# Weights joined in their load buffers, and lower halves of weights and values taken on GpSimd, in a pooled attention and bilinear MoE kernel

## The chip, the cores and the metric

The kernel runs on one core of a Trainium2 chip. The metric is the device time of one launch, in microseconds, as the median of several runs. The engines are TensorE (PE, matrix products; its weight loads are listed as PEld), VectorE (DVE), ScalarE (ACT), GpSimd (POOL) and SyncE (SP), which issues all DMAs here.

## The reference

```python
def _attn_ref(q, k, v):                      # (4, 8, 1152, 64) each, float32
    B, H, S, D = q.shape
    q_pool = q.reshape(B, H, S // 2, 2, D).mean(axis=3)
    scores = 1.0 / np.sqrt(D) * np.matmul(q_pool, k.transpose(0, 1, 3, 2))
    scores = scores - np.max(scores, axis=-1, keepdims=True)
    attn = np.exp(scores)
    attn = attn / (np.sum(attn, axis=-1, keepdims=True) + 1e-09)
    return np.matmul(attn, v).astype(np.float32)

def _moe_ref(x, w_a, w_b, w_out):            # x (2304, 512); weights float64,
    a = x @ w_a                              # (512, 1536), (512, 1536), (1536, 512)
    b = x @ w_b
    return (a * b @ w_out).astype(np.float32)

x = attn_out.transpose(0, 2, 1, 3).reshape(B * S // 2, H * D)
```

The weights arrive as float64. The kernel gets them as pairs of 32-bit words, and has to make numbers of its own formats from the two words of each.

## The kernel before

**Attention.** Work goes by pairs of heads, four to a batch, four batches. For batch 0 there are two rounds over its pairs (even rows, then odd rows); the other batches take each pair in one pass. A pass makes score blocks of 128 rows by 1152 keys on PE (`qk`; float32 for batches 0 and 1, pairs of float16 halves for 2 and 3), 144 blocks in all. `sm_max` (L750) copies a block out of PSUM on DVE and takes its maximum, `sm_exp` (L757) takes the exponent on ACT, `sm_hi` (L770, ACT) and `sm_lo` (L774, DVE) write the upper and lower float16 half of the probabilities, a DMA transposes them, and `pv` (L868) multiplies them with the halves of v. The first four passes go another way: PE transposes the float32 probabilities itself (`tr_pe`, `pv_f`). The halves of v for a pass are made from `vraw` by `v_hi` (L550, ACT) and `v_lo` (L553, DVE) into the one buffer `vs`.

**Weights.** There are 12 slices f of 128 hidden units, each with a tile of a (m = 0), of b (m = 1) and of w_out (m = 2), 512 elements a partition. For each tile SP loads the raw words into one of four buffers (`w_load`), ACT writes the scaled upper word into a separate tile z (`w_abs`, L580) and turns the lower word into the last bits (`w_tail`, L588, in place), POOL adds the sign (`w_sign`, L592), DVE joins the parts in z (`w_join`, L599) and takes the maximum (`w_mag`, L583). For a and b, `w_sum` adds the maxima over the partitions on PE, `w_scale` (L614) and `w_inv` make a scale of them, and `w_hi` (L675, ACT) and `w_lo` (L678, DVE) write the scaled upper and lower halves. For w_out the halves wait for `wo_scale`, which needs all 12 tiles.

**MoE.** The 2304 tokens form nine tiles of 256. For a tile, each f is one step: `moe_mm` (L949) makes a and b in PSUM with 24 products of halves, ACT copies a out (`moe_a`, L984), DVE multiplies (`moe_g`, L987), ACT and POOL split the result into halves (`moe_gh`, L992; `moe_gl`, L995; on DVE for the last three tiles) and `moe_o` (L1014) multiplies with w_out. The steps of tiles that are ready stand between attention's blocks on PE.

**Order.** Each piece of work is a task of class `Plan`, with an engine and names that it reads and writes. The order of each engine is written out by hand in `ORDERS`, five lists of task numbers. Each engine's queue runs in that order.

Of the kernel before, what the change touches and what calls it, by code (L numbers as in the profile page):

```python
# [217 lines left out]


class Plan:  # L220

# [4 lines left out]

    def add(self, eng, dur, key, fn, args=(), r=(), w=(), gen=0.45, block=0.0, port=None, lag=0.0, after=(), mode=0, leaves=None):  # L230
# [1035 lines left out]
```

## Time and profile before

| | us |
|---|---|
| median of 3 runs | 824.34 |
| lowest and highest | 820.56, 826.82 |
| the profiled execution | 820.92 |
| its span, first to last instruction | 819.1 |
| busy: PE, DVE, ACT, POOL | 759.3, 643.9, 567.4, 204.3 |

The span is that of one execution. Busy time counts an instruction from start to end; matmuls overlap each other, so a stretch in which PE is busy throughout can still have room. The mean granted clock of TensorE over the span is 0.977 of full speed.

### The profile page before, as it was taken

Reading aid. Unit: us, or ns where it says so; the run is one execution under the profiler, and the core shown is the slowest. Engines: PE = TensorE matmul, PEld = TensorE weight load, DVE = VectorE, ACT = ScalarE, POOL = GpSimd, SP = SyncE. Lnnn points to the kernel's source line nnn. Section 1 sums busy time; section 2 is a strip of 40 time slices with the busy share of each in tenths; the row PEclk is TensorE's granted clock in tenths of the full one; section 3 lists DMA queues with packets and bytes.
Section 4 is the critical chain, followed back from the end, with each engine's and each line's share of the span. In section 5 each row is a group of like instructions: output and inputs, shape, how many; then the busy total and the mean of one; then the engine's idle time right before and its main releaser. Section 6 shows DMA issues by size and latency. Waiting matters only on the chain.

```text
span 819.1 us, 21402 instructions
## 1 busy us (share of the span) xinstructions
PE 759.3 (93%) x8906; PEld 566.6 (69%) x8906; DVE 643.9 (79%) x1271; ACT 567.4 (69%) x940; POOL 204.3 (25%) x182
## 2 busy tenths in 40 slices
PE   7888457999999999999999999989999999999998
PEld 5665335787678775678658875867678668577775
DVE  5999999899988899999989999979788832321222
ACT  5999987688977788887878789876776752221211
POOL 4787774202311114200240204021310120000000
PEclk9998888999999999999999999999999999999999
DMA  7766778999999999999999999998897670000010
GB/s 253 268 216 206 213 225 190 175 216 193 221 188 213 178 197 195 199 201 207 192 197 168 211 209 184 196 184 175 139 179 121 128 144 2 1 26 1 1 27 26
DMA packets 316433, 132.32 MB, mean 162 GB/s; under 512 B 300848, under 2 KB 302896, under 8 KB 316336
## 3 DMA queue, kind: packets, MB, share of 16 engines
q1 hardware_dynamic: 316336, 130.96, 77.4%
q8 instruction: 69, 1.13, 0.6%
q14 instruction: 28, 0.23, 0.1%
HBM read 50.72 MB, written 4.72 MB: 68 GB/s over the span
## 4 chain that ended last, share of the span: by engine, by line
PE 32%; DVE 22%; DMA 4%; issue 4%; ACT 2%; ACTq 0%; DVEq 0%
PE ab L949 17%; DVE p L774 7%; DVE s L750 6%; PE ab L1014 5%; DMA pt<-p 4%; PE xps L868 3%; PE sps L1014 3%; PE sps L720 3%; ACT p L770 1%; DVE vs L553 1%; DVE g L987 1%; PE xps L1014 1%; DVE vmx L506 1%; DVE kmx L433 1%; DVE k L459 1%
## 5 line engine op out<-in xcount | busy, mean ns | idle before, releaser
L949 PEld LDWEIGHTS <-wab 128*128 128x128 f16 x2592 | 251.1, 98 | 37.5 <-issue 2.1
L949 PE MATMUL ab<-xt,wab 128*128 128x256 f16 x2304 | 262.6, 273 | 0.6 <-DVE o L1020 0.4
L774 DVE SCALAR_TENSOR_TENSOR p<-s,st,p 128x1152 f16<-128x1152 f32 x128 | 183.2, 1436 | 13.4 <-ACT p L770 12.9
L770 ACT ACTIVATE p<-s,st 128x1152 f16<-128x1152 f32 x128 | 158.9, 1249 | 49.2 <-DMA pt<-p 13.6
L757 ACT ACTIVATE s<-s,st 128x1152 f32<-128x1152 f32 x144 | 180.1, 1251 | 17.5 <-DVE s L750 16.3
L868 PE MATMUL xps<-pt,vs 128*64 128x128 f16 (+1 forms) x3888 | 110.1, 216 | 4.9 <-issue 2.0
L868 PEld LDWEIGHTS <-vs 128*64 128x64 f16 x3888 | 101.7, 111 | 17.2 <-issue 14.9
L750 DVE TENSOR_SCALAR_CACHE_REDUCE s<-sps 128x1152 f32<-128x1152 f32 x72 | 96.4, 1348 | 14.1 <-PE sps L718 13.9
L718 PE MATMUL sps<-k,q 64*128 64x512 f32 (+2 forms) x480 | 97.9, 542 | 10.3 <-DVE s L750 6.3
L750 DVE TENSOR_SCALAR_CACHE_REDUCE s<-sps,ksc 128x1152 f32<-128x1152 f32 x72 | 100.8, 1409 | 7.5 <-PE sps L720 6.5
L984 ACT ACTIVATE g<-ab 128x256 f32<-128x256 f32 x108 | 40.2, 375 | 95.2 <-PE ab L949 94.9
L995 POOL TENSOR_TENSOR gl<-g,gh 128x256 f16<-128x256 f32 x72 | 60.0, 839 | 181.3 <-ACT gh L992 153.3
L987 DVE SCALAR_TENSOR_TENSOR g<-ab,cc,g 128x256 f32<-128x256 f32 x108 | 51.2, 478 | 65.7 <-ACT g L984 65.6
L1014 PE MATMUL ab<-wo,gh 128*128 128x512 f16 x336 | 100.2, 380 | 1.6 <-DVE g L987 1.5
L718 PEld LDWEIGHTS sps<-k,q 64*128 64x128 f32 (+1 forms) x480 | 63.9, 190 | 45.0 <-issue 23.3
L592 POOL TENSOR_SCALAR raw<-raw 128x512 f16<-128x512 f32 x36 | 84.7, 2354 | 35.0 <-ACT raw L588 19.4
L992 ACT ACTIVATE gh<-g 128x256 f16<-128x256 f32 x108 | 43.2, 408 | 46.9 <-PE ab L1014 20.4
L720 PE MATMUL sps<-k,q 64*128 64x512 f16 (+2 forms) x720 | 66.9, 327 | 4.8 <-DVE s L750 4.2
L1014 PEld LDWEIGHTS <-gh 128*128 128x128 f16 x432 | 40.1, 100 | 41.6 <-issue 1.5
L430 POOL TENSOR_TENSOR q<-qraw 128x576 f32<-128x576 f32 (+2 forms) x20 | 27.6, 1382 | 150.5 <-PE sps L718 55.5
L1014 PE MATMUL ab<-wo,gl 128*128 128x512 f16 x168 | 63.7, 379 | 0.8 <-POOL gl L995 0.7
L720 PEld LDWEIGHTS <-q 64*128 64x128 f16 (+1 forms) x720 | 41.1, 97 | 32.8 <-issue 13.2
(126 smaller groups left out, 753.6 us busy)
## 6 DMA issues: line engine op xcount, KB each, us to landing
raw<-in_w_ab_dram SPq DMA_DIRECT2D x24, 512.0 KB, 4.2
k<-in_k_dram SPq DMA_DIRECT2D x18, 576.0 KB, 5.2
vraw<-in_v_dram SPq DMA_DIRECT2D x17, 576.0 KB, 4.5
qraw<-in_q_dram SPq DMA_DIRECT2D x12, 576.0 KB, 5.1
...
pt<-p SPq DMA_TRANSPOSE x128, 5.4
...
```

The costliest lines, as they stand in the source:

```text
L592: nc.gpsimd.tensor_scalar(out=raw_h[ri(n)], in0=raw_t[ri(n)][:, :, 1].bitcast(F32), scalar1=2.0 ** -100, scalar2=None, op0=ALU.mult)
L718: return nc.tensor.matmul(out, q, k, start=True, stop=True)
L720: return nc.tensor.matmul(out, q[:, hq], k[:, hk], start=(hq, hk) == (0, 0), stop=(hq, hk) == (1, 0))
L750: nc.vector.tensor_scalar(out=s_t[sbuf(i)], in0=sps[:, at:at + S], scalar1=-1.0 / 16.0 if u is None else ksc[:, u, 4:5], scalar2=None, op0 ...
L757: nc.scalar.activation(out=s, in_=s, func=AF.Exp, scale=-1.0, bias=t[:, 0:1], accum_out=t[:, 1:2])
L770: nc.scalar.activation(out=p_t[pbuf(i)][:, 0], in_=s_t[sbuf(i)], func=AF.Copy, scale=st_t[i % NST][:, 3:4])
L774: nc.vector.scalar_tensor_tensor(out=p[:, 1], in0=s, scalar=st_t[i % NST][:, 3:4], in1=p[:, 0], op0=ALU.mult, op1=ALU.subtract)
L868: nc.tensor.matmul(xps[half(e), at:at + w], vs[:, c, e, hv], pt[t][:, hp, c, c0:c0 + w], start=(c == 0 and n == 0), stop=(c == NCH - 1 and ...
L949: nc.tensor.matmul(dst if t < 8 else dst.rearrange("p (b n) -> p b n", b=B), wab[:, f, 1 - m, a, c], moe_x(t, b, c), start=(n == 0), stop= ...
L987: nc.vector.scalar_tensor_tensor(out=g_t[:, f], in0=ab[j][:, 0], scalar=cc[:, t, f:f + 1], in1=g_t[:, f], op0=ALU.mult, op1=ALU.mult)
L995: (nc.vector if dve else nc.gpsimd).tensor_tensor(out=gl_t[j], in0=g_t[:, f], in1=gh_t[j], op=ALU.subtract)
L1014: nc.tensor.matmul(out_bank(t, u), g[:, us], wo[:, f, a], start=(first and n == 0), stop=(last and n == 2))
```

## The change

**Weights.** The z tiles are gone, and there are seven raw buffers (two of them in the space of an x tile that is not yet in use). `w_mag` takes the maximum of the raw upper words as they were loaded; `w_real` turns it into the real one with two small operations; the scale is a power of 256 that `w_scale` makes from the exponent bits of the sum; `w_z` (ACT) multiplies the upper words by it in place; `w_join` joins in the raw buffer. The joined number is already scaled, so `w_hi` copies and `w_lo` subtracts: for a and b `w_lo` is a `tensor_tensor` on GpSimd. All tiles of a and b come before all of w_out.

**Values.** `v_mul` multiplies `vraw` by its scale in place on GpSimd, `v_hi` copies, `v_lo` is a subtraction on GpSimd.

**Order.** All five lists of `ORDERS` are new, as are some of the planner's durations; the product buffer `xps` gets its dependencies from the order of PE's list.

```diff
 ORDERS = (
     (
-        2, 3, 4, 21, 22, 5, 6, 47, 33, 35, 37, 7, 39, 41, 8, 9, 62, 156, 64, 16, 66, 68, 70, 43, 44, 167, 181, 169,
+        2, 3, 4, 5, 6, 21, 22, 7, 8, 47, 33, 35, 37, 106, 39, 41, 9, 62, 64, 138, 68, 66, 70, 149, 151, 163, 153, 43,
...
-    NRAW, NT_ = 4, 2 * B + 1
+    NRAW, NT_ = 7, 2 * B + 1
...
-    raw_t = [T(f"raw{j}", [128, 512, 2], I32) for j in range(NRAW)]
+    raw_t = [T(f"raw{j}", [128, 512, 2], I32) for j in range(NRAW - 2)]
+    raw_t += [xt[1][:, a].rearrange("p c n -> p (c n)").bitcast(I32).rearrange("p (n w) -> p n w", w=2) for a in range(2)]
...
+    def v_mul(p):
+        nc.gpsimd.tensor_scalar(out=vraw, in0=vraw, scalar1=vsc[:, p, 0:1], scalar2=None, op0=ALU.mult)
+
     def v_hi(p):
-        nc.scalar.activation(out=vs[:, :, :, 0], in_=v_heads, func=AF.Copy, scale=vsc[:, p, 0:1])
+        nc.scalar.activation(out=vs[:, :, :, 0], in_=v_heads, func=AF.Copy)
 
     def v_lo(p):
-        nc.vector.scalar_tensor_tensor(
-            out=vs[:, :, :, 1], in0=v_heads, scalar=vsc[:, p, 0:1], in1=vs[:, :, :, 0], op0=ALU.mult, op1=ALU.subtract
-        )
+        nc.gpsimd.tensor_tensor(out=vs[:, :, :, 1], in0=v_heads, in1=vs[:, :, :, 0], op=ALU.subtract)
...
     def prep_v(p, key):
-        add("ACT", 1.146, key, v_hi, (p,), r=["vraw", f"vsc{p}"], w=["vsh"])
-        add("DVE", 1.36, key, v_lo, (p,), r=["vraw", "vsh", f"vsc{p}"], w=["vsl"], port=True)
+        add("POOL", 2.4, key, v_mul, (p,), r=[f"vsc{p}"], w=["vraw"])
+        add("ACT", 1.146, key, v_hi, (p,), r=["vraw"], w=["vsh"])
+        add("POOL", 2.5, key, v_lo, (p,), r=["vraw", "vsh"], w=["vsl"])
...
-    def w_abs(f, m, n):
-        nc.scalar.activation(out=zt(f, m), in_=raw_t[ri(n)][:, :, 1].bitcast(F32), func=AF.Abs, scale=2.0 ** -112)
...
+    def w_z(f, m, n):
+        by = wz[:, 1, m, f:f + 1].bitcast(F32) if m < 2 else 2.0 ** -112
+        up = raw_t[ri(n)][:, :, 1].bitcast(F32)
+        nc.scalar.activation(out=up, in_=up, func=AF.Copy, scale=by)
...
     def w_join(f, m, n):
-        z = zt(f, m).bitcast(I32)
         nc.vector.scalar_tensor_tensor(
-            out=z, in0=z, scalar=3, in1=raw_t[ri(n)][:, :, 0], op0=ALU.logical_shift_left, op1=ALU.bitwise_or
+            out=zt(f, m).bitcast(I32), in0=raw_t[ri(n)][:, :, 1], scalar=3, in1=raw_t[ri(n)][:, :, 0],
+            op0=ALU.logical_shift_left, op1=ALU.bitwise_or
         )
...
+LO_ON = ("POOL", "POOL")
...
     def w_lo(f, m):
+        if m < 2:
+            on = nc.gpsimd if LO_ON[m] == "POOL" else nc.vector
+            on.tensor_tensor(out=w_dst(f, m, 1), in0=w_src(f, m), in1=w_dst(f, m, 0), op=ALU.subtract)
+            return
         nc.vector.scalar_tensor_tensor(
-            out=w_dst(f, m, 1), in0=w_src(f, m), scalar=w_by(f, m), in1=w_dst(f, m, 0), op0=ALU.mult, op1=ALU.subtract
-        )
+            out=w_dst(f, m, 1), in0=w_src(f, m), scalar=wr[:, 2, f:f + 1], in1=w_dst(f, m, 0), op0=ALU.mult, op1=ALU.subtract
+        )
...
     def prep_w(f, key):
-        for m in range(3):
...
         for m in range(2):
+            prep_raw(f, m, key)
...
     def prep_wo(key):
+        for f in range(NF):
+            prep_raw(f, 2, key)
+            prep_z(f, 2, key)
```

GpSimd's order before, in the rows up to the second lower half of g (`gl`). The names `raw`, `xt`, `xr` and `q` are the raw words, the halves of x and the pooled queries.

```order
L592 TENSOR_SCALAR raw_99<-raw_99 128x512
L909 TENSOR_TENSOR xt_63<-x_66,xt_63 128x256
L592 TENSOR_SCALAR raw_100<-raw_100 128x512
L592 TENSOR_SCALAR raw_101<-raw_101 128x512
L592 TENSOR_SCALAR raw_102<-raw_102 128x512
L430 TENSOR_TENSOR q_79<-qraw 128x320
L909 TENSOR_TENSOR xr<-x_66,xr 128x64
L909 TENSOR_TENSOR xt_63<-x_66,xt_63 128x256
L995 TENSOR_TENSOR gl_90<-g,gh_92 128x256
L430 TENSOR_TENSOR q_78<-qraw 128x576
L995 TENSOR_TENSOR gl_91<-g,gh_93 128x256
```

GpSimd's order now, in the rows up to the first `gl`. L620 is `w_sign`, L714 `w_lo` of a or b, L566 `v_mul`, L572 `v_lo`, and L961 the lower half of x; `xt_64` is one of the two borrowed raw buffers.

```order
L714 TENSOR_TENSOR wab<-xt_64,wab 128x512 x2
L620 TENSOR_SCALAR raw_96<-raw_96 128x512
L961 TENSOR_TENSOR xt_63<-x_66,xt_63 128x256
L566 TENSOR_SCALAR vraw<-vraw,vsc 128x1152
L620 TENSOR_SCALAR xt_64<-xt_64 128x512
L714 TENSOR_TENSOR wab<-raw_100,wab 128x512
L714 TENSOR_TENSOR wab<-raw_96,wab 128x512
L572 TENSOR_TENSOR vs<-vraw,vs 128x18x64
L620 TENSOR_SCALAR raw_98<-raw_98 128x512
L620 TENSOR_SCALAR raw_99<-raw_99 128x512
L1047 TENSOR_TENSOR gl_91<-g,gh_93 128x256
```

Before, all 36 signs are done ahead of the first `gl`. Now 26 are, and 22 lower halves of weights and the first preparation of v stand among them; the rest of w_out comes behind.

DVE's order before, around the first product g of a and b (L987). L963 and L964 make a bound of x, L967 a scale, L678 is `w_lo`, L761 and L767 are parts of the softmax sum, and `p` is a lower half of the probabilities.

```order
L963 TENSOR_SCALAR xn<-xps 128x1
L964 RECIPROCAL xn<-xn 128x1
L767 RECIPROCAL st<-st 128x1
L967 TENSOR_SCALAR cc<-wb,xn 128x4
L761 TENSOR_SCALAR st<-st 128x1
L678 SCALAR_TENSOR_TENSOR wab<-z_98,wsc,wab 128x512
L987 SCALAR_TENSOR_TENSOR g<-ab_121,cc,g 128x256
```

DVE's order now, around the same step (L1039). L626 is `w_join`, L802 `sm_max`, L826 `sm_lo`, L598 `w_mag`, and L1015, L1016 and L1019 are the bound and the scale.

```order
L626 SCALAR_TENSOR_TENSOR raw_100<-raw_100 128x512
L802 TENSOR_SCALAR s_81,st<-sps 128x1152
L1015 TENSOR_SCALAR xn<-xps 128x1
L1016 RECIPROCAL xn<-xn 128x1
L813 TENSOR_SCALAR st<-st 128x1
L826 SCALAR_TENSOR_TENSOR p_88<-s_82,st,p_88 128x1152
L626 SCALAR_TENSOR_TENSOR raw_96<-raw_96 128x512
L802 TENSOR_SCALAR s_82,st<-sps 128x1152
L1019 TENSOR_SCALAR cc<-wb,xn 128x4 x2
L1039 SCALAR_TENSOR_TENSOR g<-ab_120,cc,g 128x256
L598 TENSOR_REDUCE wmx<-raw_99 128x1
L1039 SCALAR_TENSOR_TENSOR g<-ab_121,cc,g 128x256
```

Ahead of the first g stand 36 joins and 27 score blocks before, 22 joins and 24 blocks now; the joins and maxima of w_out follow among the g steps.

## Rows read from the trace of the kernel before

**Rows 1.** The page's slices: busy tenths in 40 equal parts of the span
```profile
PE   7888457999999999999999999989999999999998
DVE  5999999899988899999989999979788832321222
POOL 4787774202311114200240204021310120000000
```

**Rows 2.** Busy time by stretch; columns in the first row
```profile
core 0: us, PE busy (x) PEld busy (x) DVE busy (x) ACT busy (x) POOL busy (x), PEclk, DMA share, GB/s
0.00:128.30 128.30, 92.18 (x683) 68.26 (x684) 114.50 (x253) 112.75 (x210) 87.62 (x50) 0.88 0.70 225
128.30:819.10 690.80, 667.10 (x8226) 498.31 (x8225) 529.44 (x1019) 454.67 (x731) 116.72 (x132) 1.00 0.80 150
160.00:660.00 500.00, 488.09 (x6541) 363.18 (x6539) 460.41 (x856) 393.48 (x602) 101.17 (x116) 1.00 1.01 187
40.00:60.00 20.00, 16.70 (x149) 13.22 (x147) 18.74 (x39) 19.62 (x42) 16.61 (x9) 0.93 0.68 235
```

**Rows 3.** Single lines: durations min/median/max in ns, first and last start
```profile
L949 PE MATMUL ab<-xt,wab x2304: 269/273/421, 128.3 to 808.3; 128*128 128x256 f16 x192
L984 ACT ACTIVATE g<-ab x108: 357/376/386, 133.8 to 808.6; 128x256 f32<-128x256 f32 x108
L987 DVE SCALAR_TENSOR_TENSOR g<-ab,cc,g x108: 462/479/485, 146.2 to 809.4; 128x256 f32<-128x256 f32 x108
L868 PE MATMUL xps<-pt,vs x3888: 189/219/314, 145.2 to 674.0; 128*64 128x128 f16 x156, 128*64 128x64 f16 x39
```

**Rows 4.** The same view: lower halves on DVE, two-input work on POOL
```profile
L678 DVE SCALAR_TENSOR_TENSOR wab<-z,wsc,wab x14: 734/742/1052, 40.5 to 183.2; 128x512 f16<-128x512 f32 x14
L553 DVE SCALAR_TENSOR_TENSOR vs<-vraw,vsc,vs x16: 1394/1410/1420, 117.5 to 650.5; 128x1152 f16<-128x1152 f32 x16
L995 POOL TENSOR_TENSOR gl<-g,gh x72: 665/672/1892, 154.6 to 664.7; 128x256 f16<-128x256 f32 x72
L430 POOL TENSOR_TENSOR q<-qraw x20: 722/1412/2526, 4.2 to 567.3; 128x576 f32<-128x576 f32 x12, 128x256 f32<-128x256 f32 x4, 128x320 f32<-128x320 f32 x4
```

**Rows 5.** Groups by line: busy us, mean ns, idle before
```profile
L592 POOL TENSOR_SCALAR raw<-raw 128x512 f16<-128x512 f32 x36 | 84.7, 2354 | 35.0 <-ACT raw L588 19.4 <-PE sps L718 9.1 <-ACT s L757 4.3
L750 DVE TENSOR_SCALAR_CACHE_REDUCE s<-sps 128x1152 f32<-128x1152 f32 x72 | 96.4, 1348 | 14.1 <-PE sps L718 13.9
L757 ACT ACTIVATE s<-s,st 128x1152 f32<-128x1152 f32 x144 | 180.1, 1251 | 17.5 <-DVE s L750 16.3
L588 ACT ACTIVATE raw<-raw 128x512 int32<-128x512 uint32 x36 | 24.5, 691 | 7.1 <-DMA raw<-in_w_ab_dram 5.8 <-DMA raw<-in_w_out_dram 1.3
L580 ACT ACTIVATE z<-raw 128x512 f32<-128x512 f32 x14 | 9.6, 688 | 0.8 <-DVE wab L678 0.8
L583 DVE TENSOR_REDUCE wmx<-z 128x1 f32<-128x512 f32 x14 | 9.3, 672 | 0.0
L614 DVE TENSOR_SCALAR wsc<-xps 128x2 f32<-128x2 f32 x12 | 1.8, 148 | 0.0
```

**Rows 6.** The timeline: three meetings of POOL and DVE; start us, us
```profile
304.75 0.67 POOL L995 TENSOR_TENSOR gl<-g,gh 128x256 f16<-128x256 f32 x1 [0.89 <-ACT gh L992]
304.78 1.85 DVE L774 SCALAR_TENSOR_TENSOR p<-s,st,p 128x1152 f16<-128x1152 f32 x1
...
407.54 1.42 DVE L774 SCALAR_TENSOR_TENSOR p<-s,st,p 128x1152 f16<-128x1152 f32 x1
407.89 1.60 POOL L995 TENSOR_TENSOR gl<-g,gh 128x256 f16<-128x256 f32 x1 [1.46 <-ACT gh L992]
...
71.88 2.29 POOL L592 TENSOR_SCALAR raw<-raw 128x512 f16<-128x512 f32 x1
72.61 0.68 DVE L599 SCALAR_TENSOR_TENSOR wo<-wo,raw 128x512 int32<-128x512 int32 x1
```

**Rows 7.** The chain that ended last: start us, us
```profile
675.80 27.61 PE ab L949 x252
```

More of the change, by code (lines that the diff above doesn't have):

```diff
@@ L232, in add @@
         deps = set(after)
+        if "xps" in w:
+            self.in_bank = n
+            self.bank[n] = []
+        elif "xps" in r:
+            self.bank[self.in_bank].append(n)
+            deps.add(self.in_bank)
+        r, w = [x for x in r if x != "xps"], [x for x in w if x != "xps"]
         for x in r:
@@ L250, in order @@
         eng, dur, _, _, _, deps, gen, block, port, lag, mode, leaves = map(list, zip(*self.tasks))
+        reads = []
+        for i in ORDERS[PE]:
+            if i in self.bank:
+                deps[i] = sorted({*deps[i], *reads})
+                reads = self.bank[i]
         assert all(eng[i] == e for e, o in enumerate(ORDERS) for i in o) and sorted(i for o in ORDERS for i in o) == list(range(n))
@@ L356 @@
     osb = [T(f"o{u}", [128, DM]) for u in range(2)]
-    z_t = osb + [T(f"z{2 + j}", [128, 512]) for j in range(NZ - 2)]
-    raw_t = [T(f"raw{j}", [128, 512, 2], I32) for j in range(NRAW)]
+    raw_t = [T(f"raw{j}", [128, 512, 2], I32) for j in range(NRAW - 2)]
+    raw_t += [xt[1][:, a].rearrange("p c n -> p (c n)").bitcast(I32).rearrange("p (n w) -> p n w", w=2) for a in range(2)]
+    raw_last = []
     xsq = T("sq", [128, B, TOK], mybir.dt.bfloat16)
-    one = T("one", [128, 1])
+    one, four = T("one", [128, 1]), T("four", [128, 1])
     vmx = T("vmx", [128, NPAIR])
@@ L628, in w_length @@
         nc.tensor.matmul(
-            xps[:, 500:500 + 2 * (f1 - f0)], one.broadcast_to([128, 128]), wsq[:, f0:f1].rearrange("p f m -> p (f m)"),
-            start=True, stop=True,
+            xps[:, 500:500 + 2 * (f1 - f0)].rearrange("p (m f) -> p m f", m=2), one.broadcast_to([128, 128]),
+            wsq[:, :, f0:f1], start=True, stop=True,
         )
@@ new lines, in prep_raw, with prep_z @@
+    def prep_raw(f, m, key):
+        n = wn(f, m)
+        rw = f"raw{ri(n)}"
+        add("SP", 1.7, key - 4, w_load, (f, m, n), w=[rw + "l", rw + "a"], lag=LOAD_LAG)
+        add("ACT", 0.555, key, w_tail, (n,), w=[rw + "l"])
+        add("POOL", 2.35, key, w_sign, (n,), r=[rw + "a"], w=[rw + "l"], port=False)
+        add("DVE", 0.6, key, w_mag, (f, m, n), r=[rw + "a"], w=[f"wmx{f}{m}"])
+    def prep_z(f, m, key):
+        n = wn(f, m)
+        z, rw = zname(f, m), f"raw{ri(n)}"
+        add("ACT", 0.55, key, w_z, (f, m, n), r=[f"wz{f}"] * (m < 2), w=[rw + "a"])
+        raw_last.append(add("DVE", 0.61, key, w_join, (f, m, n), r=[rw + "a", rw + "l"], w=[z], port=True))
@@ L697, in prep_w @@
+    def prep_w(f, key):
+        for m in range(2):
+            prep_raw(f, m, key)
+        mx = [f"wmx{f}{m}" for m in range(2)]
+        add("DVE", 0.14, key - 5, w_real, (0, 2, f, f + 1), r=mx, w=[x + "r" for x in mx])
+        add("PE", 0.2, key - 5, w_sum, (f, f + 1), r=[x + "r" for x in mx] + ["ones"], w=["xps"])
+        add("DVE", 0.26, key - 5, w_scale, (f, f + 1), r=["xps"], w=[f"wz{f}"])
+        for m in range(2):
+            prep_z(f, m, key)
             z = zname(f, m)
-            add("ACT", 0.615, key, w_hi, (f, m), r=[z, f"wsc{f}"], w=[f"w{f}{m}h"])
@@ L699, in prep_w @@
-            add("DVE", 0.68, key, w_lo, (f, m), r=[z, f"w{f}{m}h", f"wsc{f}"], w=[f"w{f}{m}l"], port=True)
+            add("ACT", 0.55, key, w_hi, (f, m), r=[z], w=[f"w{f}{m}h"])
+            on = LO_ON[m]
+            raw_last.append(add(on, 1.07 if on == "POOL" else 0.6, key, w_lo, (f, m), r=[z, f"w{f}{m}h"], w=[f"w{f}{m}l"], port=True))
     def prep_wo(key):
-        add("PE", 0.2, key, wo_sum, (), r=[f"wmx{f}2" for f in range(NF)] + ["ones"], w=["xps"])
-        add("DVE", 0.95, key, wo_scale, (), r=["xps"] + [f"wsd{f}" for f in range(NF)] + [f"wb{f}" for f in range(NF)], w=["wr"])
+        for f in range(NF):
+            prep_raw(f, 2, key)
+            prep_z(f, 2, key)
@@ L704, in prep_wo @@
+        mx = [f"wmx{f}2" for f in range(NF)]
+        add("DVE", 0.14, key, w_real, (2, 3, 0, NF), r=mx, w=[x + "r" for x in mx])
+        add("PE", 0.2, key, wo_sum, (), r=[x + "r" for x in mx] + ["ones"], w=["xps"])
+        add("DVE", 0.95, key, wo_scale, (), r=["xps"] + [f"wsc{f}" for f in range(NF)] + [f"wb{f}" for f in range(NF)], w=["wr"])
         for f in range(NF):
@@ L706, in prep_wo @@
             add("ACT", 0.615, key + f, w_hi, (f, 2), r=[z, "wr"], w=[f"w{f}2"])
-            add("DVE", 0.68, key + f, w_lo, (f, 2), r=[z, "wr"], w=[f"w{f}2"], port=True)
+            add("DVE", 0.66, key + f, w_lo, (f, 2), r=[z, "wr"], w=[f"w{f}2"], port=True)
     def sbuf(i):
@@ L933, in x_split @@
         names = [name[m] for m in which]
-        add("ACT", 0.06 * len(which) + 0.55 * n, key, x_hi, (p, j, which), r=xs, w=[x + "h" for x in names])
-        add("POOL", 0.2 * len(which) + 0.9 * n, key, x_lo, (p, j, which), r=xs + [x + "h" for x in names],
-            w=[x + "l" for x in names])
+        add("ACT", 0.06 * len(which) + 0.55 * n, key, x_hi, (p, j, which), r=xs, w=[x + "h" for x in names], after=raw_last if b == 1 else ())
+        add("POOL", 0.23 * len(which) + 1.35 * n, key, x_lo, (p, j, which), r=xs + [x + "h" for x in names],
+            w=[x + "l" for x in names], after=raw_last if b == 1 else ())
     def moe_x(t, hl, c):
@@ L1150 @@
     for n in range(IDLE):
-        add("PE", 0.44, -40 if n < 8 else 2 * (n - 8), idle, (), r=["ones"], w=["xps"])
+        add("PE", 0.44, -40 if n < 8 else 2 * (n - 8), idle, (), r=["ones"], w=["xps", "xpv"])
     prep_qk(passes[0], -20)
```

111 lines of the change are left out of this document (57 added, 54 removed), and 292 rows, old and new, of the table ORDERS.

## The prediction

> **What bounds the kernel now.** I read the page's slices first, then the busy time by stretch, then when each kind of work first starts. The slices show three regimes [rows 1]: up to about 140 us TensorE (PE) has holes while VectorE (DVE) is full; from there to 660 us both PE and DVE are full; after that only PE is. The stretches put numbers on it [rows 2]. Before the first MoE matmul, at 128.3 us [rows 3], PE is busy 92 of 128 us at a granted clock of 0.88; from then to the end it is busy 667.1 of 690.8 us, nearly all at 1.00. So two things set the end: when the MoE work starts, and how little PE waits afterwards (23.7 us now). Between 160 and 660 us DVE is busy 460 of 500 us and PE 488: relief of DVE alone can win little there, because PE, whose work the change leaves as it is, has only 12 us to give. What the change can win is mainly the start.
>
> **What is taken from DVE, and what comes instead.** Both programs have the same number of PE instructions, and 36 weight loads. DVE loses 24 lower halves of a and b (0.74 us each) and 16 lower halves of v (1.41 us) [rows 4]: 17.8 + 22.6 = 40.4 us. It gains some 36 small operations at 0.15 us [rows 5], 5 us. GpSimd (POOL) gains 24 subtractions of 512 elements, 16 multiplications and 16 subtractions of 1152. No row shows these shapes there. Its two-input rows are 0.67 us for 256 elements and 1.41 us for 576 (medians, [rows 4]), so 1.26 us for 512 between them and, carried on, 2.74 us for 1152. Its one-input row, w_sign, is dearer: 2.35 us for 512 [rows 5], which would be 5.3 us for 1152. I take 1.26 and 2.74, because the subtractions are the same operation as the cheaper rows; 2.35 and 5.3 stay as upper ends. The strided, in-place forms of the join, the maximum and w_z I cost as now: w_tail already writes with a stride and in place and takes 0.69 us, as w_abs does, which writes without one [rows 5]. If such a write did cost DVE more, each tenth of a microsecond on 24 joins would be 2.4 us.
>
> **The start.** I count what stands ahead of the first MoE step in each engine's order, before and after.
> DVE, up to the first g step (146.2 us now): 20 lower halves of weights fewer (14.8 us), one of v (1.4), 14 joins (0.68 each in the timeline [rows 6], 9.5), 12 maxima (0.67, 8.0), three blocks' score copies (1.35, 4.0) and lower halves (1.41, 4.2), the w_out scale (11 small ones, 1.7); 28 small ones more (4.2). Net 39 us less: 107 us.
> ACT, up to its first MoE copy (133.8 us now): 11 w_tail and 12 w_abs or w_z fewer, two w_hi more, all at about 0.69, and five 1152-wide passes fewer at 1.25: 21 us less, 113 us; the first matmul stands 5.5 us ahead of it, 107 us.
> POOL has more to do, not less. Ahead of the last lower half of x that the first MoE matmul needs stand 23 w_sign (2.35 us in the mean, 54), 20 new subtractions (25), 7 sums of q (0.72 at the least, about 1, 7) and 4 subtractions for x (the size of the 0.67 us row, 3): 89 us. From 8 us on that ends at 97 us if POOL never waits; at the share it reaches in a stretch where it is busiest, 16.61 of 20 us [rows 2], at 115 us. So the bound of the first stage passes from DVE to a mixture of POOL and ACT, and I take 110 us for the first MoE matmul, 18 us earlier than now; bounds 100 and 125.
>
> **The rest by PE.** The same PE work follows, 667 us. Its waits: 12 of the 23.7 us lie in 160 to 660 us, where they are DVE's pace; part goes with the relief, part returns because MoE now starts while twelve w_out tiles are still to be joined, and moe_o needs their scale. I take 20 us, bounds 12 and 35. End: 110 + 667 + 20 = 797 us of span.
>
> **The same by DVE, as a check.** From the first g step to the last product with v (146.2 to 674.0 us [rows 3]) are 527.8 us. In the new order this stretch takes over what was ahead of it (14 joins, 12 maxima, three blocks, the w_out scale: 27 us) and seven more g steps (3.4), and loses 15 lower halves of v (21.2) and four of weights (3.0): +7 us. New is that POOL's long subtractions meet DVE's two-input operations. What such a meeting costs stands in the timeline [rows 6]: a DVE lower half that began 0.03 us after a POOL subtraction of 0.67 us took 1.85 instead of 1.42 us; a POOL subtraction that began 0.35 us after a DVE one took 1.60 instead of 0.67 us; but a join that began 0.7 us into a w_sign took its usual 0.68 us. The first two waited for the end of the other, the third did not. After the first g step DVE's new order has 162 two-input operations of 512 elements or more in some 520 us, one per 3.2 us; one that falls at random into a subtraction of 2.74 us waits on average so that each subtraction costs 2.74 squared over 6.4, 1.17 us, 18 us for 15. For the multiplications, which are more like w_sign, I take nothing and keep another 18 us as the end. With the first g step at 116 us the last product with v ends at 116 + 528 + 7 + 18 = 669 us. Behind it stand 145 us now; the new order has 264 MoE matmuls fewer there (576 for 840), at 27.61 us for 252 [rows 7] 29 us. 669 + 116 = 785 us, earlier than PE's 797, so PE's sum decides.
> The Trainium skill (SBUF — State Buffer, Who interferes with whom) says that the pair of ports which DVE and GpSimd share is locked for a whole instruction, and that a DVE operation with two SBUF inputs contends with a GpSimd one that reads SBUF. It speaks against this change: by it the moved work still blocks DVE, and the multiplications would block it too. The first two meetings above agree with it; the join in w_sign does not, or not for the whole instruction. By the rule the check would be 785 + 18 = 803 us, later than the other sum, and the time 808.
>
> **Time.** The profiled run took 820.92 us for a span of 819.1, 1.8 more; the median of the three runs, 824.34, lies 3.4 us above it. 797 + 1.8 + 3.4 = **802 us**, 2.7% faster. A measurement of this kernel tells about 1% from no change.
>
> **Rivals.**
> 1. *GpSimd sets the start and takes the gain.* The queue is served in order, and w_sign's row shows 35 us of idle time ahead of it even now [rows 5]. At a share of 0.83, the first MoE matmul is as late as today when a new subtraction costs 1.75 us: 8 + (64 + 35) / 0.83 = 127 us. Then 127 + 667 + 24 + 5 = 823 us, no change; at w_sign's 2.35 us, 8 + (64 + 47) / 0.83 = 142 us and 838 us. For it: the strided source, waits of an in-order chain through four engines. Against: the 0.67 us rows. Chance 0.16, of which 0.02 slower.
> 2. *The lower halves of g stand behind v on GpSimd (the other side).* Now POOL is idle over 4/5 of the time from 128 us on (busy 117 of 691 [rows 2]) and a g subtraction starts when asked. In the new order they queue behind the two passes over v, 5.5 us, or 8.0 us with the dear multiplication, and PE, in order, has only two such buffers ahead. If PE waited 4.1 us (one subtraction of 2.74 and one DVE operation of 1.41) at each of 15 pairs, 802 + 62 = 864 us. It decides from 2.1 us a pair: 802 + 31 = 833 us, 1% slower than before. Against it: PE has products of scores and of other tiles to issue between, and the order mostly puts other rows between the two passes. Chance 0.08.
> 3. *The ports make DVE the bound.* If every one of the 15 multiplications and subtractions held up a DVE operation for its whole 2.74 us, 82 us for the 18 assumed, the check gives 849 us; with half of that, 41 us, 808, which is 813 us as a time. The first needs a meeting of full length each time, where a random one costs 1.17 us; something near the second, still faster, gets 0.10, and what lies beyond it is counted with rival 2. The rule above is of this kind.
>
> **How the numbers follow.** Forecast, 784 to 814 us: 0.66. Rival 3 near 813: 0.10. Both are faster by over 1% (below 816.1): **0.76**. Rival 1 without its end: **0.14** for within 1%. Rival 2 and the end of rival 1: **0.10** slower (above 832.6). The low end takes the first matmul at 100 us and 12 us of waits, 779 + 5 = 784; the high end must reach into rival 1, 824, which leaves out rival 2, a sliver of rival 1 and a little below 784.
>
> **What would show it.** First MoE matmul near 110 us and first g step within 10 us of it; the 512-element subtraction near 1.26 us and both passes over v near 2.7 us on POOL; PE busy about 667 us after the first MoE matmul with waits of 12 to 35 us, and no releaser in GpSimd's lines among PE's larger ones; the last product with v near 667 us or later, with DVE less full than now. I am wrong if the first matmul is later than 125 us, if PE's waits after it pass 35 us, or if w_lo takes over 1.75 us.

## The result, and the profile after

The changed kernel takes 834.31 us (median of 4 runs, 833.16 to 834.84) against 823.92 us before (4 runs, 820.56 to 826.82), a ratio of 1.0126 with the interval 1.0085 to 1.0166: slower by 1.3%. The prediction was 802 us; its sign was wrong. The profiled execution took 834.84 us for a span of 833.1.

The page's slices of the kernel after, to be laid beside [rows 1]:

```profile
PE   7887789977899997899999989899989999999998
DVE  5999889999987888877999999898998975222222
POOL 4788879884605244122431442223432430000000
```

PE's row is no longer full from 140 us on: 7s and 8s stand among its 9s up to the end of attention.

Single lines of the kernel after, columns as in [rows 3, 4]. L1001 is `moe_mm`, L1036 `moe_a`, L1039 `moe_g`, L920 `pv`, L714 `w_lo`, L566 `v_mul`, L572 `v_lo`:

```profile
L1001 PE MATMUL ab<-xt,wab x2304: 268/273/422, 116.6 to 823.5; 128*128 128x256 f16 x192
L1036 ACT ACTIVATE g<-ab x108: 357/384/386, 121.6 to 825.3; 128x256 f32<-128x256 f32 x108
L1039 DVE SCALAR_TENSOR_TENSOR g<-ab,cc,g x108: 453/483/485, 123.6 to 825.7; 128x256 f32<-128x256 f32 x108
L920 PE MATMUL xps<-pt,vs x3888: 189/219/315, 130.5 to 718.4; 128*64 128x128 f16 x156, 128*64 128x64 f16 x39
L714 POOL TENSOR_TENSOR wab<-raw,wab x18: 1153/1164/1185, 27.6 to 145.8; 128x512 f16<-128x512 f32 x18
L566 POOL TENSOR_SCALAR vraw<-vraw,vsc x16: 3187/3198/4307, 115.8 to 662.1; 128x1152 f32<-128x1152 f32 x16
L572 POOL TENSOR_TENSOR vs<-vraw,vs x16: 2369/2386/2847, 124.8 to 674.4; 128x1152 f16<-128x1152 f32 x16
```

The start is nearly as predicted: first MoE matmul at 116.6 us for 128.3 before, first g step at 123.6 for 146.2 [rows 3]. The last product with v, however, starts at 718.4 us and not at 674.0.

Busy time by stretch, after (up to the first MoE matmul, from there on, and the two fixed stretches of [rows 2]; then from the first g step to the last product with v, and from the first g step of tile 0 to that of tile 1):

```profile
0.00:116.60 116.60, 92.03 (x675) 68.72 (x676) 97.83 (x241) 96.46 (x183) 85.86 (x61) 0.88 0.66 211
116.60:833.10 716.50, 673.61 (x8233) 500.07 (x8233) 549.68 (x1027) 471.28 (x758) 236.69 (x178) 0.99 0.78 150
160.00:660.00 500.00, 464.98 (x6154) 342.79 (x6154) 445.66 (x815) 375.93 (x575) 183.18 (x144) 0.98 0.95 180
...
123.60:718.60 595.00, 556.87 (x7384) 416.64 (x7381) 514.16 (x944) 437.99 (x680) 229.10 (x173) 0.98 0.92 177
...
123.60:237.00 113.40, 97.76 (x1271) 71.37 (x1269) 106.96 (x195) 94.88 (x151) 79.58 (x47) 0.97 0.97 206
```

The last two for the kernel before, which [rows 2] do not hold:

```profile
146.20:674.20 528.00, 515.64 (x7054) 385.16 (x7048) 475.71 (x879) 409.87 (x629) 107.61 (x126) 1.00 1.00 186
...
146.20:237.70 91.50, 90.93 (x1211) 68.67 (x1206) 85.17 (x155) 75.66 (x117) 19.54 (x23) 0.99 1.05 199
```

PE's holes after the first MoE matmul grew from 23.7 to 42.9 us (716.5 - 673.6). From the first g step to the last product with v *both* engines have more time without work: PE 12.4 us before and 38.1 after, DVE 52.3 and 80.8. Two further lines show where the lead of the start went: tile 1 begins at 237.0 us, where it began at 237.7 before. All but 0.7 of the 22.6 us is gone in one tile, in which DVE is busy for 107 of 113 us.

DVE's waits from the first g step to the last product with v, in the kernel before (whom it waits for; us, times, longest):

```profile
DVE p L774 <- ACT p L770: 12.9, 13, 1.9
...
DVE g L987 <- ACT g L984: 2.3, 4, 0.7
```

and in the kernel after:

```profile
DVE g L1039 <- ACT g L1036: 24.6, 24, 4.8
DVE p L826 <- ACT p L822: 20.6, 22, 2.3
```

PE's waits after the first MoE matmul, in the kernel after:

```profile
PE sps L770 <- DVE s L802: 9.1, 8, 2.8
PE sps L772 <- DVE s L802: 7.3, 5, 2.6
PE ab L1066 <- DVE g L1039: 5.3, 1, 5.3
...
PE ab L1001 <- POOL xt L961: 1.0, 2, 0.5
```

PE waits for DVE to copy scores out, and DVE waits for a and b, which come of PE by way of ACT. GpSimd is hardly named by either. It shows in DVE's durations instead. A stretch of the timeline, kernel after: `v_mul`, and a lower half of the probabilities (1.41 us alone) that meets it.

```profile
491.20 3.19 POOL L566 TENSOR_SCALAR vraw<-vraw,vsc 128x1152 f32<-128x1152 f32 x1
...
491.52 3.85 DVE L826 SCALAR_TENSOR_TENSOR p<-s,st,p 128x1152 f16<-128x1152 f32 x1
```

The DVE operation began 0.32 us into `v_mul` and ended 0.98 us after it: it can have run only from 0.44 us before `v_mul`'s end. In every meeting with an undelayed `v_mul` in which DVE was lengthened, duration less that of the operation alone (1.41 us, or 0.74 for a lower half of w_out) puts this moment at 2.75 or 2.76 us after `v_mul`'s start. Summed over all nine meetings (one with a `v_mul` that was itself delayed) DVE's two-input operations lose 11.9 us in `v_mul`, and 3.2 in `v_lo` and 3.5 in `w_sign` in the same way. In all they took 21.4 us more than at the median of their line, where it was 6.9 before.

Operations with one input are held too. In the meeting below, a scale of k, 0.17 us alone, takes 2.98 us; the next copies of scores stand behind it on DVE, and PE waits 1.78 us for them at 529.1 us. With a second one, 1.09 for 0.22 us at 463.6 us, that is another 3.7 us, so DVE loses 15.5 us in `v_mul`.

```profile
521.84 4.24 POOL L566 TENSOR_SCALAR vraw<-vraw,vsc 128x1152 f32<-128x1152 f32 x1 [5.34 <-PE xps L456]
...
523.11 2.98 DVE L463 TENSOR_SCALAR ksc<-ksc 128x2 int32<-128x2 int32 x1
```

### The profile page after: what moved, and what is told of

Same layout as the page of the kernel before. It is cut to its first block, busy times and chain, and to the rows that moved or that the text cites. A ratio compares the mean times of both kernels' runs of the same rounds, so it can differ in the third digit from the quotient of the medians.

```text
span 833.1 us, 21433 instructions
## 1 busy us (share of the span) xinstructions
PE 765.6 (92%) x8906; PEld 568.8 (68%) x8906; DVE 647.5 (78%) x1267; ACT 567.7 (68%) x940; POOL 322.6 (39%) x238
## 5 line engine op out<-in xcount | busy, mean ns | idle before, releaser
L1001 PEld LDWEIGHTS <-wab 128*128 128x128 f16 x2592 | 251.9, 99 | 43.4 <-issue 4.1
L1001 PE MATMUL ab<-xt,wab 128*128 128x256 f16 x2304 | 264.4, 274 | 5.4 <-DVE g L1039 4.3
L826 DVE SCALAR_TENSOR_TENSOR p<-s,st,p 128x1152 f16<-128x1152 f32 x128 | 194.8, 1526 | 21.0 <-ACT p L822 20.6
L920 PE MATMUL xps<-pt,vs 128*64 128x128 f16 (+1 forms) x3888 | 108.7, 216 | 7.1 <-DMA pt<-p 3.9
L1039 DVE SCALAR_TENSOR_TENSOR g<-ab,cc,g 128x256 f32<-128x256 f32 x108 | 51.0, 479 | 81.5 <-ACT g L1036 80.8
L920 PEld LDWEIGHTS <-vs 128*64 128x64 f16 x3888 | 101.7, 112 | 17.7 <-issue 15.7
L770 PE MATMUL sps<-k,q 64*128 64x512 f32 (+2 forms) x480 | 97.4, 540 | 16.9 <-DVE s L802 13.9
L1066 PE MATMUL ab<-wo,gh 128*128 128x512 f16 x336 | 102.3, 386 | 6.6 <-DVE g L1039 5.3
L802 DVE TENSOR_SCALAR_CACHE_REDUCE s<-sps 128x1152 f32<-128x1152 f32 x72 | 96.7, 1350 | 14.1 <-PE sps L770 13.8
L802 DVE TENSOR_SCALAR_CACHE_REDUCE s<-sps,ksc 128x1152 f32<-128x1152 f32 x72 | 100.9, 1412 | 7.2 <-PE sps L772 6.1
L1036 ACT ACTIVATE g<-ab 128x256 f32<-128x256 f32 x108 | 39.7, 375 | 89.9 <-PE ab L1001 89.7
L770 PEld LDWEIGHTS sps<-k,q 64*128 64x128 f32 (+1 forms) x480 | 63.0, 189 | 52.3 <-issue 25.1
L1044 ACT ACTIVATE gh<-g 128x256 f16<-128x256 f32 x108 | 43.5, 407 | 47.4 <-PE xps L1066 18.7
L566 POOL TENSOR_SCALAR vraw<-vraw,vsc 128x1152 f32<-128x1152 f32 x16 | 53.3, 3331 | 39.3 <-DVE st L813 18.0
L620 POOL TENSOR_SCALAR raw<-raw 128x512 f16<-128x512 f32 x26 | 62.0, 2384 | 15.7 <-ACT raw L616 7.0
L772 PEld LDWEIGHTS <-q 64*128 64x128 f16 (+1 forms) x720 | 40.7, 97 | 36.8 <-issue 17.6
```

The costliest lines, as they stand in the source:

```text
L566: nc.gpsimd.tensor_scalar(out=vraw, in0=vraw, scalar1=vsc[:, p, 0:1], scalar2=None, op0=ALU.mult)
L620: nc.gpsimd.tensor_scalar(out=raw_h[ri(n)], in0=raw_t[ri(n)][:, :, 1].bitcast(F32), scalar1=2.0 ** -100, scalar2=None, op0=ALU.mult)
L770: return nc.tensor.matmul(out, q, k, start=True, stop=True)
L772: return nc.tensor.matmul(out, q[:, hq], k[:, hk], start=(hq, hk) == (0, 0), stop=(hq, hk) == (1, 0))
L802: nc.vector.tensor_scalar(out=s_t[sbuf(i)], in0=sps[:, at:at + S], scalar1=-1.0 / 16.0 if u is None else ksc[:, u, 4:5], scalar2=None, op0 ...
L826: nc.vector.scalar_tensor_tensor(out=p[:, 1], in0=s, scalar=st_t[i % NST][:, 3:4], in1=p[:, 0], op0=ALU.mult, op1=ALU.subtract)
```

## The experiments

Each is the kernel after with one edit, if nothing else is said. "Tile 1" is the start of its first g step.

**1 to 4. Which of the moved operations costs?** The multiplication on ACT, at the place in ACT's order directly ahead of `v_hi`:

```diff
-        nc.gpsimd.tensor_scalar(out=vraw, in0=vraw, scalar1=vsc[:, p, 0:1], scalar2=None, op0=ALU.mult)
+        nc.scalar.activation(out=vraw, in_=vraw, func=AF.Copy, scale=vsc[:, p, 0:1])
...
```


> The multiplication of v by its scale moves from GpSimd to ScalarE, directly ahead of the upper half of v; all else is the changed kernel. Lock theory (in the changed kernel the 16 multiplications of 3.2 us hold up DVE's two-input operations for nearly their whole length, 12 us in all, and PE waits behind DVE): those 12 us and the PE waits at those places go, 812 to 822 us. Order theory (the loss is the late w_out and the new order, the ports are a side matter): 829 us or more. Delay theory (what hurts is the long chain multiply, upper half, lower half before the products with v, not the ports): the chain gets 2 us shorter of 7, so about a third of the loss comes back, 828 to 831 us.

v prepared as before (no `v_mul`, the scale in `v_hi`), weights and order as after (`v_lo` on DVE where its inputs are ready):
```diff
...
-        nc.gpsimd.tensor_tensor(out=vs[:, :, :, 1], in0=v_heads, in1=vs[:, :, :, 0], op=ALU.subtract)
+        nc.vector.scalar_tensor_tensor(
+            out=vs[:, :, :, 1], in0=v_heads, scalar=vsc[:, p, 0:1], in1=vs[:, :, :, 0], op0=ALU.mult, op1=ALU.subtract
+        )
...
```


> v is prepared as before the change (no multiplication on GpSimd, scale in the upper half, lower half as one DVE operation of 1.41 us); weights and order stay changed. DVE gets 22 us of work back. Lock theory: the 15 us that DVE lost to long GpSimd passes go and 22 us of work come, so little changes on DVE, while GpSimd's chain is gone: 820 to 832 us. Order theory: 835 us or more, since DVE has more to do and the order is as bad. First MoE matmul near 117 us by both.

The lower halves of a and b on DVE, v as after:
```diff
-LO_ON = ("POOL", "POOL")
+LO_ON = ("DVE", "DVE")
...
```


> The lower halves of a and b go back to DVE as plain subtractions (24 of about 0.7 us), v stays on GpSimd. If the weights' part is what makes the start earlier, the first MoE matmul moves from 117 us back to 125 to 135 us and the time to 840 to 850 us. If GpSimd set the start, taking 28 us from it leaves the first MoE matmul where it is or earlier, and the time at 830 to 836 us.

Both of the last two edits:

> Both moves to GpSimd are undone; the joined-in-place weights, w_out last and the new order stay, with the 40 DVE operations put in where their inputs are ready. Lock theory: 832 to 845 us, DVE has 40 us more than in the changed kernel and 15 us fewer waits. Order theory: the same or more, 840 to 855 us.

| | us | ratio to before | first MoE matmul | tile 1 |
|---|---|---|---|---|
| 1 `v_mul` on ACT | 828.42 | 1.007 (1.004 to 1.010) | 116.7 | 236.8 |
| 2 v on DVE | 833.84 | 1.012 (1.007 to 1.017) | 114.9 | 240.1 |
| 3 `w_lo` on DVE | 846.43 | 1.027 (1.021 to 1.034) | 126.8 | 251.0 |
| 4 both on DVE | 839.75 | 1.020 (1.015 to 1.026) | 126.3 | 251.4 |

The lower halves of the weights on GpSimd are worth, in this order, what experiment 3 expected of them: without them the start is 10 us later and the time 12 us longer (6 between 2 and 4). v on GpSimd is worth nothing in this order: with 16 more operations of 1.41 us on DVE the second kernel is as fast. And taking `v_mul` alone off GpSimd gains 6 us, which is in the range of the delay theory (828 to 831), not of the lock theory; 15 to 18 come back to that. From tile 0 to tile 1 all four take 113 to 117 us.

**5 to 7, 9, 10. Which engine sets which stretch?** My theory was that each stretch goes by the larger need: DVE up to tile 1, TensorE after. Work that nobody waits for is added, or work is left out. 5, 16 us more for DVE before tile 1:
```diff
+        for _ in range(3 if m == 2 else 1):
             nc.vector.tensor_reduce(out=wmx[:, m, f:f + 1], ...
```


> The maximum of the raw words of each w_out tile is taken three times instead of once: 24 more VectorE instructions of 0.67 us, 16 us, at 124 to 162 us, in the stretch between the first two tiles of g steps. They read SBUF alone, write a few bytes and nobody else waits for the second and third. Theory A (each stretch takes the larger of what VectorE and TensorE need in it, and from 123 to 237 us that is VectorE): the whole is 11 to 16 us longer than the changed kernel's 834.3, 845 to 850 us, and the second tile's first g step comes 11 to 16 us later. Rival B (what is lost is PE's ledger with waits for GpSimd, and VectorE has room): at most 4 us, below 839 us. Rival C (the ports alone): no change, since these instructions take no second input from SBUF.

6, 16 us more for DVE after it:
```diff
+        for _ in range(2 if p >= 4 else 1):
             nc.vector.tensor_reduce(out=vmx[:, p:p + 1], in_=vf[j], ...
```


> The maximum of v is taken twice from the second batch on: 12 more VectorE instructions of 1.34 us, 16 us, at 210 to 650 us, the same sum as in the kernel with the maxima of w_out three times. Theory A (from 240 to 690 us TensorE is the larger need, VectorE 393 of 450 us busy): 0 to 6 us over the changed kernel's 834.3, 834 to 840 us. Rival D (VectorE is one chain from the first g step to the last product with v, as my check took it, whatever the stretch): 12 to 16 us, 846 to 850 us.

7, less for DVE before tile 1 (`w_mag` and `w_join` of w_out over 8 of 512 columns, 12.3 us less by the trace; the columns left out are filled at the very start, while DVE has nothing else to do):
```diff
...
+        w = 8 if m == 2 else 512
-            ... in_=raw_t[ri(n)][:, :, 1].bitcast(F32), ...
+            ... in_=raw_t[ri(n)][:, 0:w, 1].bitcast(F32), ...
...
```


> Left out: the maximum and the join of the w_out tiles are done over 8 of 512 columns, so the output is not the reference's (w_out's other columns are a constant). VectorE has 14 us less at 124 to 220 us, all else is as in the changed kernel. Theory A (VectorE sets that stretch): 9 to 14 us under the changed kernel's 834.3, 820 to 825 us, with the second tile's first g step that much earlier than 237. Rival B (TensorE's waits for GpSimd and its cold clock set the stretch): at most 4 us, 830 to 834 us. Rival C (ports): 24 meetings of a join with a GpSimd instruction at most, some 3 us, 831 us.

9, some 13 us more for TensorE after tile 1 (its busy time grew by 15.5):
```diff
+        if 1 <= t <= 5:
+            todo = todo[:1] + todo
...
```


> The first product of every a and b of tiles 1 to 5 is done twice: 120 more matmuls of 256 columns, each followed by the next after 0.11 us, 13 us more for TensorE between 230 and 690 us, nothing more for the others. VectorE's 16 us in the same stretch cost 15 us in full. Theory G (TensorE and VectorE each wait for the other in turn, so that work added to either lies on the path): 10 to 13 us over the changed kernel's 834.3, 844 to 848 us. Rival D (VectorE alone is the chain there): 0 to 5 us, 834 to 839 us.

10, less for DVE after tile 1 (12.8 us by the trace, 12 maxima at 0.28 for 1.34 us):
```diff
+        x = vf[j] if p < 4 else vf[j][:, 0:1]
-        nc.vector.tensor_reduce(out=vmx[:, p:p + 1], in_=vf[j], ...
+        nc.vector.tensor_reduce(out=vmx[:, p:p + 1], in_=x, ...
```


> Changed: the maximum of v is taken over 64 of 1152 elements a partition from the second batch on, so the scale of v is made from a part of it; VectorE has 12 times 1.24 us, 15 us less at 210 to 650 us. Theory G (both engines are on the path in turn): part of it comes back, 4 to 9 us, 825 to 830 us, as 14 us fewer in the early stretch gave 7. Rival D (VectorE alone is the chain): 12 to 15 us, 819 to 822 us. Rival A (TensorE is the larger need there): 0 to 3 us, 831 to 834 us.

| | work, us | time, us | against 834.31 | tile 1 |
|---|---|---|---|---|
| 5 | DVE +16 before tile 1 | 848.22 | +13.9 | 251.7 |
| 6 | DVE +16 after it | 849.58 | +15.3 | 240.5 |
| 7 | DVE -12 before it | 827.55 | -6.8 | 230.8 |
| 9 | PE +13 after it | 843.27 | +9.0 | 238.1 |
| 10 | DVE -13 after it | 832.70 | -1.6 | 236.6 |

The first half of the theory stands: before tile 1, DVE's time counts (5; and 7, with half of what was taken). The second half fell with 6: DVE's 16 us after tile 1 cost 15 too (two of the twelve operations stand ahead of it, which shows in tile 1's 3.5 us), although TensorE's 13 us there cost 9. Neither engine alone is the bound. Work added to either costs most of its length. Work taken from DVE alone after tile 1 brings back 1.6 us, which cannot be told from nothing: the four runs of 10 lie between 830.67 and 838.78. Two engines that run down one interleaved order, each waiting for the other by turns, would do this; but theory G, which says so, forecast 825 to 830 us for 10 and missed, so that account is argued and not shown.

**8, 11 to 14. The order.** 8 is kernel 1 (`v_mul` on ACT) with the five lists put anew for the written durations, 12 the same for the durations of the trace; 11 has the operations of the changed kernel, 14 those of kernel 2, and 13 those of the kernel *before*, all three put anew as 12. The edit is the table alone, of 12:
```diff
+ORDERS = (
+    (
+        2, 3, 4, 5, 6, 21, 22, 7, 8, 47, 33, 35, 37, 39, 41, 106, 62, 64, 138, 68, 66, 9, 70, 149, 151, 163, 153, 43,
...
```


> The multiplication of v on ScalarE, as in the first experiment (828.4 us), with the five orders put anew for that: the operations are the same, only their places differ, so that joins and maxima of w_out stand less densely between the first and second tile of g steps. Theory A (the loss lies in which engine's work stands in which stretch): 808 to 818 us, faster than before by 1% or so. Rival E (the loss lies in the operations themselves: more DVE and GpSimd work, ports): 824 to 832 us, as that experiment.

> The changed kernel's operations, all on the engines where the change put them (v's multiplication and lower half on GpSimd), with the five orders put anew for the durations that the trace shows (v's multiplication 3.2 us where the program writes 2.4, the second scaling of the upper words 0.66 for 0.55, GpSimd's lower halves of weights 1.2 for 1.07). Theory H (what was lost is the order: the two in-order engines wait for each other because the order was put for other durations): 812 to 822 us, with VectorE's waits for the copies of a well below 24.6 us. Rival E (the operations on GpSimd and the ports cost it): 828 to 835 us.

> The multiplication of v on ScalarE as in the first experiment, the orders put anew for the durations that the trace shows, early ones above all (the kernel with v's multiplication on ScalarE and new orders, 820.9 us, was put for the written ones). Theory H: 811 to 818 us, and the best of all here. Rival E: 820 to 828 us.

> The kernel before, with its operations unchanged and only its five orders put anew in the same way as those of the 817.5 us kernel. If that kernel's gain comes of the order alone: 812 to 819 us. If the weights' new way (the lower halves of a and b on GpSimd, the MoE work 10 us earlier) has a part in it: 819 to 826 us.

> The changed kernel with v prepared as before (lower half on VectorE, the scale in ScalarE's copy; no multiplication on GpSimd), orders put anew. Theory L (what GpSimd's passes over v cost through the ports is more than the 22 us of VectorE work they save): 815 to 822 us, about the 817.5 us of the kernel that keeps the subtraction of v on GpSimd, and 20 us under the 842.5 us of the one that keeps both passes there. Rival (VectorE's work counts in full): 832 us or more.

| operations | us | ratio to before |
|---|---|---|
| 8 `v_mul` on ACT | 820.92 | 0.996 (0.993 to 0.998) |
| 12 `v_mul` on ACT | 817.52 | 0.993 (0.989 to 0.997) |
| 14 v on DVE | 815.06 | 0.992 (0.989 to 0.994) |
| 13 kernel before | 817.35 | 0.994 (0.990 to 0.997) |
| 11 changed kernel | 842.52 | 1.022 (1.017 to 1.027) |

With equal care for the order the change's weights (14) and the weights of before (13) cannot be told apart. The order by itself is worth much: 14 has the operations of kernel 2 and takes 18.8 us less, 12 those of kernel 1 and takes 10.9 less, while the kernel before gains some 6 us by it (13). (8, at 820.92, lies between the ranges of both its theories.) Theory H, that the order alone had cost the time, fell with 11 all the same: in an order put in the same way as those of 12 and 14 the changed kernel's own operations got 8 us slower. They take 25 us more than 12, from which they differ by `v_mul`'s engine, and by the lists, each put for its own operations. This points at `v_mul` on GpSimd; the next experiments leave the lists alone.

**15, 16. Hold, or lateness?** ACT multiplies as in 1, and in `v_mul`'s old place GpSimd works on a spare buffer of zeros, once in float32 in place, once in w_sign's form.
```diff
...
+        for n in (768, 384):
+            x = spare[:, 0:n]
+            nc.gpsimd.tensor_scalar(out=x, in0=x, scalar1=vsc[:, p, 0:1], scalar2=None, op0=ALU.mult)
```


> The order of the changed kernel; ScalarE multiplies v directly ahead of its upper half (as in the first experiment, 828.4 us), and in the multiplication's old place GpSimd multiplies a spare buffer of zeros in place, float32, 768 and then 384 elements, 3.2 us together, which nobody uses. Theory L (the ports): VectorE's operations are held as in the changed kernel, about 10 us of lengthened two-input operations, 832 to 836 us. Rival T (the multiplication was late in its own chain): 826 to 830 us, as the first experiment.


```diff
...
+        x = spare.rearrange("p (n w) -> p n w", w=2)[:, :, 1]
+        y = spare.bitcast(F16).rearrange("p (n h) -> p n h", h=4)[:, :, 1]
+        for _ in range(2):
+            nc.gpsimd.tensor_scalar(out=y, in0=x, scalar1=vsc[:, p, 0:1], scalar2=None, op0=ALU.mult)
```


> As the kernel with the spare buffer multiplied in float32, but GpSimd's instruction has w_sign's form (every second float32 read, a float16 written with a stride), twice 384 elements, about 3.4 us together. w_sign held VectorE for only some 0.5 of its 2.3 us in the traces. Theory L: few operations are held, 827 to 830 us, as the first experiment. Rival (any busy GpSimd, or its queue, delays the rest): 832 to 836 us.

830.51 us (1.010, 1.007 to 1.013) and 833.31 us (1.013, 1.009 to 1.017). By time alone this was a miss: 15 lies between its two ranges, and 16 in that of the rival, by which any busy GpSimd delays the rest. The traces say more: neither held DVE for long, 1.1 and 0.8 us in all, and from tile 1 to tile 8 both ran as kernel 1 (538.0 and 539.9 us for its 538.5, where the changed kernel takes 545.5); what they lost, they lost nearly all ahead of tile 1 (238.9 and 242.6 us), and why there stays open. The long lock that I had meant to build was none. The same meeting as above, in the kernel with the spare float32 multiplication:

```profile
490.94 2.20 POOL L569 TENSOR_SCALAR spare<-spare,vsc 128x768 f32<-128x768 f32 x1
...
491.26 1.78 DVE L831 SCALAR_TENSOR_TENSOR p<-s,st,p 128x1152 f16<-128x1152 f32 x1
```

DVE was let in 0.7 us after the beginning of this one. So the price might lie in the length of the single instruction, and 17 and 18 split it, in the changed kernel and in 11.

**17, 18. The same multiplication in two halves.**
```diff
-        nc.gpsimd.tensor_scalar(out=vraw, in0=vraw, scalar1=vsc[:, p, 0:1], scalar2=None, op0=ALU.mult)
+        flat = vraw.rearrange("p c n -> p (c n)")
+        for x in (flat[:, 0:576], flat[:, 576:1152]):
+            nc.gpsimd.tensor_scalar(out=x, in0=x, scalar1=vsc[:, p, 0:1], scalar2=None, op0=ALU.mult)
```


> The changed kernel with v's multiplication on GpSimd split into two of 576 elements, about 1.65 us each (between the spare ones of 384 and 768, 1.24 and 2.20 us). Theory L (the long instruction holds VectorE for 2.8 of its 3.2 us, the short ones for some 0.5 us each): what VectorE's operations lose in it falls from 11.9 to 2 to 4 us, and the time to 826 to 830 us. Rival S (each half holds VectorE nearly to its end, as the whole does): 832 to 836 us.

> The same split in the kernel whose orders were put anew with both passes over v on GpSimd (842.5 us). Theory L: 820 to 830 us, near the 817.5 us of the kernel that differs from it by ScalarE's multiplication. Rival S, or a cause other than the hold: 838 to 844 us.

824.11 us (1.001, 0.998 to 1.004) for 834.31, and 824.88 us (1.001, 0.999 to 1.003) for 842.52: 10 and 18 us less by cutting one instruction in two. The same meeting in 17, and two of its lines:

```profile
486.77 3.54 POOL L568 TENSOR_SCALAR vraw<-vraw,vsc 128x576 f32<-128x576 f32 x2
...
486.97 1.75 DVE L828 SCALAR_TENSOR_TENSOR p<-s,st,p 128x1152 f16<-128x1152 f32 x1
```

```profile
L568 POOL TENSOR_SCALAR vraw<-vraw,vsc x32: 1715/1723/2826, 114.5 to 652.5; 128x576 f32<-128x576 f32 x32
...
L828 DVE SCALAR_TENSOR_TENSOR p<-s,st,p x128: 1393/1414/1910, 86.5 to 691.0; 128x1152 f16<-128x1152 f32 x128
```

GpSimd works even longer (1.72 us twice, for 3.20), and no lower half of the probabilities takes more than 1.91 us, where the longest took 3.85. DVE's loss in `v_mul` falls from 15.5 to 1.3 us (two-input operations 11.9 to 0.9, one-input ones 3.7 to 0.5). In 11 it is 18.4 us, 6.2 of them in three one-input operations, and in 18 it is 2.0. So 14 us less of it gave 10.2 us of time in one order, and 16 less gave 17.6 in the other; the lists, the engines and the work are the same within each pair. Lateness, in whose range 1 had come out, is not what the split takes away: the two halves together take longer than the whole, and in the changed kernel `v_hi` waits for `v_mul` only 1.4 us in all 16 passes:

```profile
L569 ACT ACTIVATE vs<-vraw 128x1152 f16<-128x1152 f32 x16 | 18.5, 1155 | 2.7 <-POOL vraw L566 1.4 <-PE xps L920 1.3
```

18 still takes 7 us more than 12. Between the two profiled runs 8.2 of 9.4 us are there when tile 1 begins (241.7 for 233.5); no run separates what makes them.

## Why the prediction was wrong

**The start: right.** 116.6 us within the bounds 100 to 125 (I took 110), the g step 7 us behind it, and GpSimd did not set it: its subtraction took 1.16 us for my 1.26, and with this work taken from it (3) the start came later, not earlier. Experiments 3 and 4 show that 10 us of the lead are due to the lower halves on GpSimd. The 6.6 us that were missing are part of the miss. DVE's own sum was further off: the first g step, at 107 us in it, came at 123.6, and DVE's busy time ahead of that step fell by 27.2 us (131.9 to 104.7) and not by 39. The small operations for the weights' scales, 28 more at 0.15 us, 4.2 us, were 27 more and took 11.8 us longer. The first of `w_real` took 0.46 us in the median:

```profile
L604 DVE TENSOR_SCALAR wmx<-wmx x13: 149/455/1256, 15.0 to 163.0; 128x2 f32<-128x2 f32 x12, 128x12 f32<-128x12 f32 x1
```

**The sum by PE: the waits failed.** "I take 20 us, bounds 12 and 35": they were 42.9, with 6.5 us more busy time beside them, at a granted clock of 0.99 for 1.00 (0.98 for 1.00 from 160 to 660 us). So the miss of the span, 833.1 for 797, is 6.6 + 6.5 + 22.9 = 36 us.

**First failed step: "For the multiplications, which are more like w_sign, I take nothing".** `v_mul` takes 3.20 us for the 2.74 assumed and holds DVE for 2.76 of them; its price in this order is 10.2 us (17). The end of 18 us that I kept for it in the DVE check would have covered DVE's loss in it, 15.5 us. There the Trainium skill (SBUF — State Buffer, Who interferes with whom) was the better guide: its lock for a whole instruction agrees nearly with `v_mul` and with `v_lo` (a meeting in 8, 2.18 of 2.38 us). It does not agree with the shorter ones: 0.53 of 1.72 us for 576 elements, 0.7 of 2.20 for 768. I had weighed the rule by one meeting with w_sign, in which the join began 0.73 us into it, when w_sign no longer held DVE (it does so for some 0.5 us), and took one form's price for another's. The term for `v_lo`, 18 us, erred the other way: 3.2 us. So the two terms together, 18 us, were nearly right (18.7), by luck, and this step alone would not have moved the forecast: it only entered a sum that I then set aside.

**Second failed step: "earlier than PE's 797, so PE's sum decides".** I made two sums, one for each engine from end to end, and took the later. For DVE I counted +7 us of work and +18 of holds from the first g step to the last product with v, 553 us; the stretch took 595. DVE's busy time rose by 38.5 us, some 19 of it work (twelve more g steps for the seven that I counted, and small operations) and some 19 lengthened operations, and its time without work rose by 28.5, though PE had holes as well. That last term I had at nothing, and PE's waits at less than half. Each engine waited for the other, and a sum for one of them, with the other's work as cover, counts none of that. Experiments 6 and 9 agree with it: work added to either is paid for the most part. Why the waits grew is shown in part: 17 puts 10.2 us down to the hold, the rest goes with the order (2 and 14, 1 and 12) and was not taken apart. Also the lead was counted as kept. "Part returns because MoE now starts while twelve w_out tiles are still to be joined" was given a few microseconds of PE's waits; in fact nearly the whole 22.6 us were back at tile 1. There the joins, maxima and lower halves of w_out stood in a stretch in which DVE had little room (5 and 7).

**The rivals.** Rival 1 (GpSimd sets the start) and rival 2 (g behind v) did not come: the first MoE matmul kept its lead, and none of PE's larger waits names a lower half of g. Rival 3 had the mechanism, with the multiplication instead of all passes. But at the price that it had, the change would still have been faster. The slower side came from the sum of both failed steps, and there 0.10 was too little.

Even with the hold taken out (17) the change gains nothing, 1.001; from tile 1 to the end that kernel needs 587.0 us of its span, the kernel before 581.4. How much of these 6 us is the order and how much the remaining holds was not measured apart; that with new orders 14 and 13 come out alike speaks for the order, but 18, with the operations of 17 in a new order, is no faster than 17.
